# Gated attention and its feed-forward on one core: the values computed transposed, with V as the loaded weight and the squares streamed

## The chip, the cores and the metric

The kernel runs on one core of a Trainium2 chip. The metric is the time of one execution in microseconds (us) on the device; runs of the kernel before took 1242.19, 1242.97 and 1243.57 us, median 1242.97 us.

## What is computed

For each of 8 batches with S = 3008 rows, u and v have 256 columns and z has 64. The first half of the kernel makes x from them, the second half is a feed-forward over all 24064 rows of x:

```python
scores = (1.0 / S) * np.matmul(z, z.transpose(0, 2, 1))
attn = np.maximum(scores, 0.0) ** 2
x = u * np.matmul(attn, v)          # then as 24064 rows of 256
h = x @ w_in                        # 256 -> 2048
g = h * (1.0 / (1.0 + np.exp(-1.702 * h)))
out = g @ w_out                     # 2048 -> 256
```

All inputs and the output are float32; the kernel's products take float16.

## The kernel before, in words

**Tiles.** Each batch's rows are cut into NIS = 6 units of 512 query rows, 48 units in all; the last unit of a batch has only 448 rows (it is called short here). The key rows are cut into NJ = 24 blocks of 128. Every matmul has a contraction of 64: the 128 rows of the array are used as two halves of 64, which work on two matmuls at a time (a pair) and add into two PSUM banks, g = 0 and 1. The two banks are added later.

**Scores.** `scores` (L286) computes for a unit n and a pair t of key blocks the scores transposed: keys on the partitions, 512 queries along the row. `relu` (L335) takes them out of PSUM on ACT or DVE, `squared` (L315) squares them in place in float16, L318 on ACT or L320 on DVE. Since the scores are symmetric, from unit 3 on the squares for earlier key blocks are not computed again: they are earlier squares, turned by a DMA transpose (tiles T, L256), and part of the diagonal block comes likewise from a half block (`mirror`, L271).

**Values, before.** `values` (L444) multiplies squares and V: a block of squares, 128 keys by 128 queries, is the loaded weight, and 256 columns of V are streamed (L457). The result, O, has queries on the partitions. A unit has 24 key blocks, 4 blocks of queries and 2 halves of the array: 192 matmuls of 256 columns; h = 0 and 1 are the two pairs of query blocks. `halves` (L512) does the last key block. In a short unit the fourth query block has 64 rows; `shorts` (L524) does it with 128 rows by 64 columns of the array (L532), and the two halves of its result are joined by a small DMA (`two`, L506) and an add (L501).

**Out of PSUM.** `both_sums` (L424) copies the two banks into a tile `sums` (L436 on ACT or L438 on DVE; 3 such tiles rotate), POOL adds the two copies (L431). For O, POOL then multiplies with u (`gate`, L473) into X. X has rows on the partitions; the feed-forward needs it the other way round, so `turn_x` (L354) turns it with DMA transposes (L367, L374) into the ring XT, and `swap_x` (L378) copies it with its two partition halves exchanged into XS (L385).

**Feed-forward.** `hidden` (L537) makes 2 x 128 of the 2048 hidden columns for a block m of 512 rows with eight matmuls of 512 columns (L547) into hg; ACT's sigmoid (L554) and DVE's multiply (L558) make GT. `outs` (L574) multiplies GT by W2 (L585, 256 columns streamed) into yps, which leaves by `both_sums` too, and is stored (L602). hg and the scores share two PSUM tiles, tag A; O and yps share four banks, tags B00 to B11.

**Order.** The program is written out by a planner that runs when it is built: it keeps one clock for each engine (`now`), a table of assumed costs (`cost`, L138), and a list of PE work (`work`, L610: O of unit n, then yps of block n - 3). Scores and hg are put in between where an engine is free. Work for ACT and DVE goes to whichever the planner has earlier, POOL's to POOL; DMAs that SP issues wait in a list (`sends`) and go out in the order of their due unit. The resulting order on each engine is fixed: an instruction that waits holds all that stand behind it on its engine.

Of the kernel before, what the change touches and what calls it, by code (L numbers as in the profile page):

```python
# [9 lines left out]
F16 = mybir.dt.float16  # L10
P = 128
# [3 lines left out]
def kernel(  # L15
# [41 lines left out]
    NG = 8  # L57

# [20 lines left out]
    RU = [const.tile([P, NIB, D], F32, name=f"RU{i}") for i in range(2)]  # L79
    for i in range(2):  # L80
        pool.memset(RU[i][SREM:, NIB - 1, :], 0.0)

# [18 lines left out]
    def load_u(n):  # L101
        b, isup = divmod(n, NIS)
        rows(b, u, isup * NIB, (isup + 1) * NIB, RU[n % 2], sp, 1)

# [11 lines left out]
    def turn_z(b, q):  # L116
# [25 lines left out]
        ("sp", "turn"): 1.45, ("sp", "mirror"): 1.3, ("sp", "turn_x"): 2.6, ("sp", "turn_z"): 2.2, ("sp", "store"): 0.6, ("sp", "swap"): 1.2,  # L142
# [143 lines left out]
    def scores(k):  # L286

        nonlocal nxt
        for i in range(k):
# [25 lines left out]
            def squared(e, at, n=n, t=t, a=a, isup=isup, cols=cols):  # L315
# [5 lines left out]
                if isup == NIS - 1 and t == NP - 1:  # L321
                    pool.memset(a[:, 1, ISUP - SREM:], 0.0)
                    at += 0.5
# [25 lines left out]
    Os, Ys, GTs, Xs = {}, {}, {}, {}  # L349
# [4 lines left out]
    def turn_x(n, at):  # L354
        b, isup = divmod(n, NIS)
        X = Xs.pop(n)
        t0 = b * S + isup * ISUP
        end = min(t0 + ISUP, (b + 1) * S)
        for c in range(NK):
            k = 0  # L360
            while t0 + k < end:
                p0 = (t0 + k) % RING
                room = min(end - t0 - k, RING - p0)
                r0, blk = k % P, k // P
                if r0 == 0 and room >= P:
                    nb = room // P
                    sp.dma_start_transpose(  # L367
                        XT[:, c, p0:p0 + nb * P].rearrange("p (n t) -> p n t", t=P),
                        X[:, c, blk:blk + nb, :].rearrange("p n d -> p (n d)"),
                    )  # L370
                    k += nb * P
                else:
                    r = min(room, P - r0)
                    sp.dma_start_transpose(XT[:, c, p0:p0 + r].unsqueeze(1), X[r0:r0 + r, c, blk, :])  # L374
                    k += r
        send(at + T_DMA, "swap", n + 1, lambda at: swap_x(t0, end, at))
# [13 lines left out]
    def squares_of(n, j, ib):  # L390

        J = j // NIB
        if turned_from(n, J):
            return T[(n, J)][:, ib, j % NIB, :]
        a = A[(n, j // 2)]
        if mirrored(n, j // 2) and ib < NIB // 2:
            return a[:, 0, (2 * ib + j % 2) * P:(2 * ib + j % 2 + 1) * P]
        if J == n % NIS and n >= NMIR:
            return by_halves(a)[:, j % 2, ib // 2, ib % 2 * P:(ib % 2 + 1) * P]
        return a[:, j % 2, ib * P:(ib + 1) * P]  # L400
# [20 lines left out]
    def take_banks(h, name):  # L421
        set_bank(h, None)
        return [psB.tile([P, 2, D], F32, name=f"{name}{g}{h}", tag=f"B{g}{h}") for g in range(2)]

    def both_sums(ps, h, scale, at, then):

        s_ = pb.tile([P, 2, 2, D], F32, name="sums", tag="sums", bufs=3)
        done = []

        def add(e, at):  # L430
            pool.tensor_tensor(s_[:, 0, :, :], s_[:, 0, :, :], s_[:, 1, :, :], ALU.add)  # L431
            then(s_[:, 0, :, :], at)

        def leave(g, e, at):
            if e == "act":
                act.activation(s_[:, g, :, :], ps[g], AF.Copy, scale=scale)  # L436
            else:
                dve.tensor_scalar(s_[:, g, :, :], ps[g], scale, None, ALU.mult)  # L438
            done.append(at)
            if len(done) == 2:  # L440
                set_bank(h, max(done))
                push(max(done), "add", ("pool",), add)

        for g in range(2):  # L444
            push(at, "part", BOTH, lambda e, at, g=g: leave(g, e, at))

    def values(n, js, h, ends):
        V = V16[n // NIS % 2]
# [3 lines left out]
        short = h == 1 and n % NIS == NIS - 1  # L452
        for j in js:
            for i2 in range(1 if short else 2):
                sq = squares_of(n, j, 2 * h + i2)
                for g in range(2):
                    pe.matmul(  # L457
                        O[g][:, i2, :], half(sq, g), half(V[:, j, :], g),
                        start=(j == 0 and i2 == 0), stop=(ends and j == js[-1] and (i2 == 1 or short)),
                    )  # L460
        at = pe_at(H, T_MM * (1 if short else 2) * len(js))
        if h == 1 and (not short or js[0] >= NJ - TAIL):
            for j in js:
                drop(n, j)
        if ends:
            if h == 0:
                assert n - 2 not in Xs
                Xs[n] = pb.tile([P, NK, NIB, P], F16, name="X", tag="X")
            O, X, R = Os.pop((n, h)), Xs[n], RU[n % 2]
            both = None  # L470

            def gate(ib, k, p=P):
                pool.tensor_tensor(  # L473
                    X[:p, :, ib:ib + k, :].rearrange("p c n d -> p n c d"),
                    both[:p, ib - 2 * h:ib - 2 * h + k, :].rearrange("p n (c d) -> p n c d", c=NK),
                    R[:p, ib:ib + k, :].rearrange("p n (c d) -> p n c d", c=NK),
                    ALU.mult,
                )

            def gone(at):  # L480
                if h == 1:
                    send(at, "turn_x", n, lambda at: turn_x(n, at))
                    if n + 2 < NU:
                        send(at, "store", n + 1, lambda at: load_u(n + 2))

            def summed(s_, at):
                nonlocal both
                both = s_
                if not short:
                    def mul(e, at):  # L490
                        gate(2 * h, 2)
                        gone(at)

                    push(at, "gate", ("pool",), mul)
                    return


                two = pb.tile([H, D], F32, name="two", tag="two", bufs=1)

                def add(e, at):  # L500
                    pool.tensor_tensor(both[:H, 1, :], both[:H, 1, :], two, ALU.add)  # L501
                    gate(3, 1, H)
                    gone(at)

                def move(at):
                    sp.dma_start(two, both[H:, 1, :])  # L506
                    push(at + 2.0, "gate", ("pool",), add)

                push(at, "gate", ("pool",), lambda e, at: gate(2, 1))
                send(at, "store", 0, move)  # L510

            both_sums(O, h, 1.0, at, summed)  # L512

    def halves(n):

        V = V16[n // NIS % 2]
        for q in range(NIB // 2):
            for g in range(2):
                pe.matmul(  # L519
                    Os[(n, g)][g][:, q, :], half(squares_of(n, NJ - 1, 2 * g + q), g), half(V[:, NJ - 1, :], g),  # L520
                    start=False, stop=False,
                )
        pe_at(H, 2 * T_MM)
        drop(n, NJ - 1)  # L524

    def shorts(n):

        V = V16[n // NIS % 2]
        O = Os[(n, 1)][0]
        for j in range(NJ - 1):  # L530
            c0 = j % 2 * SREM
            pe.matmul(  # L532
                O[c0:c0 + SREM, 1, :], squares_of(n, j, NIB - 1)[:, :SREM], V[:, j, :],
                start=False, stop=False, tile_position=(0, c0),
            )
        pe_at(0, T_MM * NJ / 2)
        for j in range(NJ - TAIL):  # L537
            drop(n, j)
# [27 lines left out]
    def last_out(Y, r0):  # L566

        o = pb.tile([P, 2, 2, D], F32, name="sums", tag="sums", bufs=3)
        for i2 in range(2):
            act.activation(o[:, 1, i2, :], Y[1][:, i2, :], AF.Copy, scale=1.0 / FSC)  # L570
            dve.scalar_tensor_tensor(o[:, 0, i2, :], Y[0][:, i2, :], 1.0 / FSC, o[:, 1, i2, :], ALU.mult, ALU.add)
            sp.dma_start(out[(r0 + i2) * P:(r0 + i2 + 1) * P, :], o[:, 0, i2, :])

    def outs(m, fg, h):  # L574
# [6 lines left out]
        for e, i2 in [(x, y) for x in range(2) for y in range(2)] if not end else [(0, 0), (1, 0), (0, 1), (1, 1)]:  # L581
            ff = fg + e * NFG
            s = 2 * h + i2
            for g in range(2):
                pe.matmul(  # L585
                    Y[g][:, i2, :], half(GT[:, e, s * P:(s + 1) * P], g), half(W2[:, ff, :], g),
# [5 lines left out]
        if end:  # L592
# [7 lines left out]
            def summed(s_, at):  # L600
                def store(at):
                    sp.dma_start(out.rearrange("(n p) c -> p n c", p=P)[:, r0:r0 + 2, :], s_)  # L602
# [4 lines left out]
            both_sums(Y, h, 1.0 / FSC, at, summed)  # L607
# [4 lines left out]
    for n in range(NTB + LAG):  # L612
        m = n - LAG
        if n < NU:
# [6 lines left out]
            for h in range(2):  # L621
                for j in range(NJ - TAIL, NJ - 1):
                    if j == NJ - 2 and h == 0:
                        work.append(("r", n, [NJ - 1]))
                        if n % NIS == NIS - 1:
                            work.append(("s", n, list(range(NJ - 1))))
# [5 lines left out]
    spans = {"r": 2 * T_MM, "s": T_MM * NJ / 2, "y": 4 * T_MM}  # L632
    before = [0.0]
    due = {}
    for i, w in enumerate(work):
        before.append(before[-1] + (2 * T_MM * len(w[2]) if w[0] == "o" else spans[w[0]]))
# [17 lines left out]
    at(0, 12, lambda: load_u(0))  # L654
    at(0, 13, load_w1, lambda: load_u(1))
# [154 lines left out]
```

## Time and profile before

| what | value |
|---|---|
| time, median of 3 runs | 1242.97 us |
| the profiled execution's own time | 1240.06 us |
| its span, first to last instruction | 1238.1 us |
| granted TensorE clock | 0.999 |
| PE busy | 1219.2 us, 18600 matmuls |
| PEld (weight loads) busy | 1018.0 us |
| DVE, ACT, POOL busy | 908.7, 810.3, 476.0 us |
| DMA: moved, mean rate | 167.25 MB, 135 GB/s |

The span lies 2 us inside the profiled execution's time, and that lies 2.9 us below the median. The busy time of a matmul is modelled and contains its latency (a pair overlaps), so that the pace of PE is read from the starts of matmuls, or from the chain of work, not from the mean of one.

### The profile page before, as it was taken

The numbers are of one execution on the slowest core, as the hardware profiler recorded it, in microseconds if no ns is written. First come the engines' busy times: TensorE is split into PE (matmuls) and PEld (weight loads), VectorE is DVE, ScalarE is ACT, GpSimd is POOL, SyncE is SP. The second block draws the span as 40 slices with busy tenths as digits, with TensorE's granted clock in tenths as the row PEclk, the third lists the DMA queues.
The fourth block names the chain that finished last, engine by engine and source line by source line (L and its number), as shares of the span: only waits on it lengthen the run. The fifth ranks groups of instructions, "written<-read, shape, count | busy, mean of one in ns | idle before, by whom it ended". The sixth has DMA issues, their size and how long they took to land.

```text
span 1238.1 us, 42078 instructions
## 1 busy us (share of the span) xinstructions
PE 1219.2 (98%) x18600; PEld 1018.0 (82%) x18600; DVE 908.7 (73%) x891; ACT 810.3 (65%) x948; POOL 476.0 (38%) x489
## 2 busy tenths in 40 slices
PE   8898999999999999999999999999999999999998
PEld 6787988887888878888988887888878888988886
DVE  8966777667876778767787677876777777777656
ACT  8865776566666666666666676666766666666544
POOL 5533343423443243433444333433434333422331
PEclk9999999999999999999999999999999999999999
DMA  9999797976888669795699946989559985685511
GB/s 166 167 169 167 139 139 137 165 125 117 142 162 153 109 117 146 132 191 105 117 148 178 144 96 125 156 128 179 103 115 172 164 132 109 134 155 100 97 45 60
DMA packets 465654, 167.25 MB, mean 135 GB/s; under 512 B 375360, under 2 KB 465472, under 8 KB 465472
## 3 DMA queue, kind: packets, MB, share of 16 engines
q1 hardware_dynamic: 414048, 147.14, 65.2%
q0 software_dynamic: 51424, 17.44, 14.0%
q8 instruction: 145, 2.38, 0.8%
q14 instruction: 37, 0.30, 0.1%
HBM read 60.29 MB, written 24.64 MB: 69 GB/s over the span
## 4 chain that ended last, share of the span: by engine, by line
PE 88%; DVE 1%; ACT 1%; issue 1%; DVEq 0%
PE O L457 33%; PE hg L547 25%; PE yps L585 24%; PE sc L301 4%; PE O L532 1%; PE O L519 1%; DVE GT L558 0%; DVE ap__6020 L320 0%; DVE ap__18204 L320 0%; DVE ap__12112 L320 0%; DVE sums L438 0%; DVE ap__21289 L339 0%; DVE ap__3546 L339 0%; DVE ap__9105 L339 0%; DVE ap__15197 L339 0%
## 5 line engine op out<-in xcount | busy, mean ns | idle before, releaser
L558 DVE TENSOR_TENSOR GT<-hg,tsg 128x1024 f16<-128x1024 f32 x376 | 453.6, 1219 | 220.4 <-ACT tsg L554 215.7
L554 ACT ACTIVATE tsg<-hg 128x1024 f16<-128x1024 f32 x376 | 378.3, 1022 | 283.6 <-PE hg L547 279.7
L431 POOL TENSOR_TENSOR sums<-sums 128x512 f32<-128x512 f32 x188 | 248.7, 1325 | 681.2 <-DVE sums L438 431.1
L547 PE MATMUL hg<-XT,W 64*128 64x512 f16 x1504 | 383.5, 376 | 2.3 <-DVE GT L558 2.0
L585 PE MATMUL yps<-W,GT 64*128 64x256 f16 x6016 | 380.8, 269 | 4.7 <-ACT sums L436 3.7
L547 PE MATMUL hg<-XS,W 64*128 64x512 f16 x1504 | 367.7, 376 | 0.0
L585 PEld LDWEIGHTS <-GT 64*128 64x128 f16 x6016 | 327.0, 94 | 42.8 <-issue 4.4
L547 PEld LDWEIGHTS <-W 64*128 64x128 f16 x3008 | 174.7, 94 | 88.8 <-issue 3.0
L457 PE MATMUL O<-V,T 64*128 64x256 f16 x3392 | 217.0, 269 | 0.0
L457 PEld LDWEIGHTS <-T 64*128 64x128 f16 x3392 | 185.9, 94 | 24.3
L473 POOL TENSOR_TENSOR X<-sums,RU 128x512 f16<-128x512 f32 (+2 forms) x104 | 138.7, 1334 | 7.5
L301 PE MATMUL sc<-ZT 64*128 64x512 f16 (+1 forms) x688 | 122.3, 363 | 5.4 <-DVE ap__832 L339 1.7
L436 ACT ACTIVATE sums<-yps 128x512 f32<-128x512 f32 x115 | 66.0, 594 | 38.9 <-PE yps L585 29.4
L436 ACT ACTIVATE sums<-O 128x512 f32<-128x512 f32 x110 | 63.3, 596 | 33.1 <-PE O L457 24.2
L438 DVE TENSOR_SCALAR sums<-O 128x512 f32<-128x512 f32 x82 | 55.6, 685 | 20.6 <-issue 9.9
L438 DVE TENSOR_SCALAR sums<-yps 128x512 f32<-128x512 f32 x69 | 47.4, 687 | 14.7 <-issue 10.1
L301 PEld LDWEIGHTS <-ZT 64*128 64x128 f16 x688 | 40.0, 94 | 12.1 <-issue 8.2
L87 POOL DMA_DIRECT2D V<-in_v_dram x32 | 28.0, 877 | 0.0
L119 POOL COPY z<-z 128x384 f16<-128x384 f16 x28 | 13.8, 493 | 0.0
L87 POOL DMA_DIRECT2D z<-in_z_dram x7 | 10.9, 1563 | 1.0 <-issue 1.0
L532 PE MATMUL O<-V,T 128*64 128x256 f16 x160 | 10.3, 275 | 0.0
L532 PEld LDWEIGHTS <-T 128*64 128x64 f16 x160 | 8.1, 110 | 1.7 <-issue 1.7
(1538 smaller groups left out, 1474.6 us busy)
## 6 DMA issues: line engine op xcount, KB each, us to landing
out_dram<-sums SPq DMA_DIRECT2D x92, 256.0 KB, 4.2
RU<-in_u_dram SPq DMA_DIRECT2D x40, 512.0 KB, 4.5
V<-in_v_dram POOLq DMA_DIRECT2D x24, 384.0 KB, 7.3
XS<-XT SPq DMA_DIRECT2D x60, 128.0 KB, 4.1
RU<-in_u_dram SPq DMA_DIRECT2D x8, 384.0 KB, 3.7
z<-in_z_dram POOLq DMA_DIRECT2D x7, 368.0 KB, 8.9
V<-in_v_dram POOLq DMA_DIRECT2D x8, 320.0 KB, 8.3
XT<-X SPq DMA_TRANSPOSE x144, 2.5
```

Source lines behind the costliest of these rows:

```text
L87: eng.dma_start(dst[:, :full - lo, :], dram[b, lo * P:full * P].rearrange("(n p) d -> p n d", p=P),)
L301: pe.matmul(sc[:, g, cols], Z[h0:h0 + DQK, 2 * t + g, :], Z[h0:h0 + DQK, isup * NIB + low:(isup + 1) * NIB, :], start=True, stop=True,)
L431: pool.tensor_tensor(s_[:, 0, :, :], s_[:, 0, :, :], s_[:, 1, :, :], ALU.add)
L436: act.activation(s_[:, g, :, :], ps[g], AF.Copy, scale=scale)
L438: dve.tensor_scalar(s_[:, g, :, :], ps[g], scale, None, ALU.mult)
L457: pe.matmul(O[g][:, i2, :], half(sq, g), half(V[:, j, :], g), start=(j == 0 and i2 == 0), stop=(ends and j == js[-1] and (i2 == 1 or short)),)
L473: pool.tensor_tensor(X[:p, :, ib:ib + k, :].rearrange("p c n d -> p n c d"), both[:p, ib - 2 * h:ib - 2 * h + k, :].rearrange("p n (c d) - ...
L532: pe.matmul(O[c0:c0 + SREM, 1, :], squares_of(n, j, NIB - 1)[:, :SREM], V[:, j, :], start=False, stop=False, tile_position=(0, c0),)
L547: pe.matmul(hg[:, e, :], half(W1[:, fg // 2, c, fg % 2 * P:(fg % 2 + 1) * P], e), half(x[:, c // 2, p0:p0 + TB], e), start=(c == 0), stop= ...
L554: act.activation(tsg, hg, AF.Sigmoid, scale=1.702 / FSC)
L558: dve.tensor_tensor(GT, hg, tsg, ALU.mult)
L585: pe.matmul(Y[g][:, i2, :], half(GT[:, e, s * P:(s + 1) * P], g), half(W2[:, ff, :], g), start=(fg == 0 and e == 0 and i2 == 0), stop=(end ...
```

## The change

The product is written the other way round. V is the loaded weight now: for a key block j and a half h of V's columns, 128 columns of V are loaded, and the squares of all the unit's queries are streamed, 512 wide. So h now stands for a half of the columns, and O has columns of V on its partitions and queries along the row: x transposed. The multiplication with u writes straight into the ring XT; `turn_x` and X are gone, `swap_x` stays. In a short unit 448 queries are streamed, and `shorts`, `two` and the memset of the padding are gone. Where the unit's squares do not lie in one pattern, they are streamed in two pieces, each with its own weight load (256 + 256 on the diagonal, 384 + 64 from the tiles T of a short unit, 256 + 192 on the diagonal of a short unit).

u must be transposed for this and is float32, while the DMA transpose takes 16-bit elements. So POOL splits each unit's u into its low and high 16-bit halves (`split_u`), two DMA transposes turn them (`turn_u`), and POOL puts them together again (`merge_u`). One tile of each kind exists; `u_did` has each step wait for the one before it and for its tile: load n for split n - 1; split n for load n and turn n - 1; turn n for split n and merge n - 1; merge n for turn n and the multiplication (gate) n - 1. The `sums` tiles become 4.

```diff
+    NSUM = 4
-    RU = [const.tile([P, NIB, D], F32, name=f"RU{i}") for i in range(2)]
+    RU = const.tile([P, NIB, D], F32, name="RU")
+    UH = const.tile([P, 2, NIB * D], U16, name="UH")
+    UHT = const.tile([P, 2, NIB, NK, P], U16, name="UHT")
+    UT = const.tile([P, NK, ISUP], F32, name="UT")
...
+    def split_u(n):
+        for w in range(2):
+            pool.tensor_copy(UH[:, w, :], RU.bitcast(U16).rearrange("p n (x w) -> p w (n x)", w=2)[:, w, :])
+
+    def turn_u(n):
+        for w in range(2):
+            sp.dma_start_transpose(UHT[:, w, :, :, :].rearrange("p n c r -> p (n c) r"), UH[:, w, :])
+
+    def merge_u(n):
+        for w in range(2):
+            pool.tensor_copy(
+                UT.bitcast(U16).rearrange("p c (n r w) -> p w n c r", n=NIB, w=2)[:, w, :, :, :], UHT[:, w, :, :, :],
+            )
...
-        ("sp", "turn"): 1.45, ("sp", "mirror"): 1.3, ("sp", "turn_x"): 2.6, ("sp", "turn_z"): 2.2, ("sp", "store"): 0.6, ("sp", "swap"): 1.2,
+        ("sp", "turn"): 1.45, ("sp", "mirror"): 1.3, ("pool", "split"): 2.2, ("pool", "merge"): 2.2, ("sp", "turn_u"): 2.9, ("sp", "turn_z"): 2.2, ("sp", "store"): 0.6, ("sp", "swap"): 1.2,
...
-    def turn_x(n, at):
...
-    def squares_of(n, j, ib):
+    def squares_of(n, j):
+        J, g, w = j // NIB, j % 2, width(n)
         if turned_from(n, J):
-            return T[(n, J)][:, ib, j % NIB, :]
+            t = T[(n, J)][:, :, j % NIB, :]
+            return [t] if w == ISUP else [t[:, :w // P, :], t[:, w // P, :w % P]]
...
+    def add_values(O, n, j, V, g, first, last):
+        c0 = 0
+        for k, x in enumerate(squares_of(n, j)):
+            w = x.shape[1] if len(x.shape) == 2 else x.shape[1] * x.shape[2]
+            o = O[:, c0:c0 + w]
+            yield o if len(x.shape) == 2 else o.rearrange("p (n r) -> p n r", n=x.shape[1]), V, half(x, g), first and c0 == 0, last and c0 + w == width(n)
+            c0 += w
...
         for j in js:
-            for i2 in range(1 if short else 2):
-                sq = squares_of(n, j, 2 * h + i2)
-                for g in range(2):
-                    pe.matmul(
-                        O[g][:, i2, :], half(sq, g), half(V[:, j, :], g),
-                        start=(j == 0 and i2 == 0), stop=(ends and j == js[-1] and (i2 == 1 or short)),
-                    )
+            both = [add_values(O[g], n, j, half(V[:, j, h * P:(h + 1) * P], g), g, j == 0, ends and j == js[-1]) for g in range(2)]
+            for pair in zip(*both):
+                for o, vj, x, first, last in pair:
+                    pe.matmul(o, vj, x, start=first, stop=last)
...
-            def gate(ib, k, p=P):
-                pool.tensor_tensor(
-                    X[:p, :, ib:ib + k, :].rearrange("p c n d -> p n c d"),
...
+                def gate(e, at):
+                    k = 0
+                    while k < w:
+                        p0 = (t0 + k) % RING
+                        r = min(w - k, RING - p0)
+                        pool.tensor_tensor(XT[:, h, p0:p0 + r], s_[:, k:k + r], UT[:, h, k:k + r], ALU.mult)
+                        k += r
+                    if h == 1:
+                        u_did("gate", n, at)
+                        send(at, "swap", n + 1, lambda at: swap_x(t0, t0 + w, at))
+
+                if u_done["merge"] >= n:
+                    push(at, "gate", ("pool",), gate)
+                else:
+                    waiting_gates.append((n, at, gate))
...
-    def shorts(n):
...
-    at(0, 12, lambda: load_u(0))
-    at(0, 13, load_w1, lambda: load_u(1))
+    at(0, 12, lambda: u_did("gate", -1, now["pe"]))
+    at(0, 13, load_w1)
```

## The prediction

> **What bounds the kernel now.** I read first the page's busy times, then the share by stages, then the waits of PE, then the chain of work inside one stage. The stages:
>
> ```profile
> PE 1219.2 (98%) x18600; PEld 1018.0 (82%) x18600; DVE 908.7 (73%) x891; ACT 810.3 (65%) x948; POOL 476.0 (38%) x489
> ```
>
> ```profile
> 0.00:60.00 60.00, 53.58 (x784) 44.12 (x785) 53.73 (x59) 50.63 (x57) 33.89 (x43) 1.00 1.23 168
> 60.00:130.00 70.00, 64.54 (x954) 52.32 (x955) 49.62 (x49) 41.02 (x49) 23.98 (x32) 1.00 1.02 165
> 130.00:1225.00 1095.00, 1093.38 (x16753) 915.81 (x16749) 799.23 (x778) 714.26 (x839) 418.15 (x415) 1.00 0.77 133
> ```
>
> Columns: PE, PEld, DVE, ACT, POOL busy, granted clock, DMA share, GB/s. From 130 us on PE never rests. Before that it rests 6.4 and 5.5 us; up to 60 us DVE is as busy as PE (53.7 of 60 us). So what PE streams counts in full, and a helper engine counts only where it makes PE wait. PE's waits, first up to 60 us, then from 60 to 130:
>
> ```profile
> PE sc L301 <- DVE ap__832 L339: 1.7, 1, 1.7
> PE sc L301 <- DVE ap__496 L339: 1.4, 1, 1.4
> ```
>
> ```profile
> PE yps L585 <- ACT sums L436: 3.7, 1, 3.7
> PE hg L547 <- DVE GT L558: 2.0, 2, 1.5
> ```
>
> The pace of PE, from the chain in a dense stage (start, length, matmuls), and its passage through `shorts`:
>
> ```profile
> 601.18 0.86 PE hg L547 x8
> 602.05 0.44 PE O L457 x8
> ```
>
> ```profile
> 278.79 1.43 PE O L532 x23
> ```
>
> Eight matmuls of 512 columns take 0.86 us, eight of 256 take 0.44; over all starts in the trace a pair of 512 takes 215.8 ns, a pair of 256 takes 109.2. That is 0.416 ns a column and 2.6 ns for each start.
>
> **Streaming, -6.8 us.** By the written order of the changed kernel its O takes 1740 pairs of 512, 7 of 448, 320 of 384, 320 of 64, 329 of 256 and 49 of 192 columns; before it was 4328 pairs of 256 and 184 matmuls of `shorts`. Where two pairs of 256 become one of 512, one start goes: 1740 x 2.6 ns = 4.5 us. In a short unit a key block costs 162.4 + 29.3 = 191.7 ns for each half of the columns; before it was 3.5 pairs for two halves, 191.1 each: nothing gained. But `shorts` takes 1.43 us where 23 x 54.6 ns = 1.26 are streamed, and by the starts there is another 0.1 us of standstill ahead of it: 0.28 us for each of 8 units, 2.3 us. Two costs are not in the trace. A matmul of 64 columns with its own weight load: a load is busy 94 ns, but wherever PE restarts after a wait the second load of a pair begins 1 ns after the first matmul and its own matmul 4 to 5 ns after that, so I take no cost beyond the stream; the far bound is a whole load not hidden, 65 ns on 320 pairs, +20.8 us. And a stream in four runs of 128 elements (tiles T, 1048 pairs), where every stream today is one run: I take nothing, since the nearest rows, 256 and 512, differ only by columns and starts; the bound is a start for each run, 3 x 2.6 ns x 1048 = +8.2 us. Neither can go below nothing: the columns and the starts are counted already.
>
> The Trainium skill, "TensorE: Matmul & The Clock Gate", section "Back-to-back issue gap", speaks against the narrow pieces: in a stream of load and matmul it gives about 81 ns per matmul at 128 columns. The trace has that stream: the 24 transposes of z (L689), 128 columns and a load each, start 53 to 56 ns apart. By the page's 81 ns a pair of 64 would lose at least 52 ns, 16.5 us on 320; by the row, nothing.
>
> **The stall at 101 us, -3.7 us.** PE's longest wait is for ACT, and ACT and DVE wait there 4.5 and 4.1 us for an out store: with three `sums`, O of h = 1 takes the tile of the yps just stored, and SP issued those stores late (100.3 us). With four, it takes a tile that a gate has freed a unit earlier. I count the 3.7 as gone.
>
> **POOL, +3 us in the long stage.** Added are 192 copies (two splits, two merges, 48 units) of 1024 elements; gone are 16 short adds and gates and 8 memsets. The rows:
>
> ```profile
> L431 POOL TENSOR_TENSOR sums<-sums 128x512 f32<-128x512 f32 x188 | 248.7, 1325 | 681.2 <-DVE sums L438 431.1 <-ACT sums L436 224.3 <-DMA T<-ap__21358 12.9
> L119 POOL COPY z<-z 128x384 f16<-128x384 f16 x28 | 13.8, 493 | 0.0
> L237 POOL COPY scrap<-V 1x2 f16<-1x2 f16 x2 | 0.3, 174 | 8.8 <-DVE V L320 7.7 <-ACT V L318 1.0
> ```
>
> From 174 ns for 2 elements and 493 for 384, a copy of 1024 takes 1.03 us; that it steps over every second half-word no row shows. From below it can't be under z's 0.49 us, from above at the two-input rate of L431 it is 2.48. I take 1.03, the row of the same kind: 198 us, POOL at some 54%. POOL's own time is hidden: XS of a block was issued 4 to 44 us ahead of its first hg. What isn't hidden is DVE's squares:
>
> ```profile
> L320 DVE TENSOR_TENSOR GT<-GT 128x1024 f16<-128x1024 f16 x4 | 2.6, 680 | 0.0
> L320 DVE TENSOR_TENSOR ap__736<-ap__736 128x1024 f16<-128x1024 f16 x1 | 1.8, 1758 | 0.0
> ```
>
> The same square, once alone, once beside POOL's work. The 54 squares that touch no POOL instruction average 0.689 us, all 179 take 169.3 us: 46 us more than alone, for 407 us of POOL arithmetic, 0.11 us for each. 198 us more make 22 us on DVE. DVE has that room (73% busy), but the two PSUM tiles of tag A are handed on closely: of 636 handovers after 130 us, 111 come less than 0.6 us before PE needs them, and 74 of these have a square in the 3.5 us before. So about 4 in 10 of the 22 us fall where it matters, and a third of it gets through the slack: +3 us; bounds 0 and, with copies of 2.48 us, +11.
>
> The Trainium skill, "SBUF — State Buffer", section "Who interferes with whom", says that VectorE with two SBUF inputs and GpSimd's reads exclude each other for a whole instruction. By that a square meets one of the 192 copies about 28 times (179 squares x 198 us / 1238) and waits half a copy, 15 us on DVE instead of 22: a third less of the term. The trace agrees in kind: DVE's multiply L558, one of whose inputs is PSUM, takes 1.21 to 1.23 us beside POOL or not.
>
> **The start, +4 us.** Up to 60 us DVE sets the pace and the DMA share is 1.23: transposes of T<-V and T<-GT take 8.3 us to land there. The first x now needs load, split, turn and merge of u in this stage. On SP, turn 0 stands behind the six T<-V, which ended at 33.8 us; landed at some 42 to 45, merged by 47. Behind the merge stand on POOL W2's load, split 1 (2.1 us) and the two gates (2.7): 53.3 us. XS(0) stands behind turn 1 on SP: issued at 54 against 47.5 us, landed after 4 to 5 us at 58 to 59, while the first hg came at 55.5. That is 3 us of wait. POOL is then busy almost to 72 us, and some four more squares slow by 0.8 us each; 1.7 us of this go into a wait that PE has at 59 us anyway. 3 + 3 - 1.7 makes 4; bounds -1 (transposes at the 4.0 us that they take on the median) and +12 (each of three units adds a landing of 4 us to POOL's chain).
>
> **The rest at nothing.** SP: 144 transposes of X (some 1.2 us to issue) and 8 small copies go, 96 of u (1.3 us, as T) come; behind them stand mirrors and T, and the mirrors have 7 to 32 us from issue to first use. DMA: 96 x 1024 packets of 256 bytes replace 48,000, and at 27 ns a packet 16 engines get 85 us more, a share of 0.84 instead of 0.77 in the long stage; if a T came late it would cost PE up to a landing, but PE waits for no DMA today. ACT and DVE copies keep their size. The end keeps its work; XS is ready sooner by the turn of X.
>
> **Sum.** 1240.06 - 4.5 - 2.3 - 3.7 + 3 + 4 = 1236.6 us for the profiled execution; that execution lies 2.9 us below the median of runs, so **1239.5 us**.
>
> **The rivals.** (A) Both added costs are hidden: squares slow only where DVE has room and merge 0 comes in time. Then 1240.06 - 10.5 + 2.9 = 1232.5. For it: PE doesn't wait for today's slowed squares after 130 us; against: the closeness of the handovers. (B) Costs and gains cancel: start and squares cost 10.5 us instead of 7, what the gains are: 1243. For it: both are terms of a chain that DVE and DMA already fill. (C) Slower: POOL becomes the brake, through the half-word copies. At 2.48 us each POOL has 476 us more, DVE 54; 11 us get through after 130 us, and the start costs 10, since the four copies ahead of the first gates are 1.45 us longer each: 1240.06 - 10.5 + 21 + 2.9 = 1253.5. It decides from about 1.8 us a copy. For it: no row shows such a copy; against: the copy row. (D) The narrow pieces pay a whole weight load: 1239.5 + 20.8 = 1260; against it the 4 to 5 ns after restarts. By the 81 ns of the Trainium skill ("TensorE: Matmul & The Clock Gate", "Back-to-back issue gap") the same rival would give 1256. (E) The streams in runs cost a start each: 1239.5 + 8.2 = 1247.7. That the change doesn't do what it says I rule out: the written order holds the counts above and no turn of X.
>
> **How the numbers follow.** Forecast, 1235 to 1240.5: 0.33. A, 1230 to 1235: 0.15. B, 1240.5 to 1245.5: 0.20. C: 0.21, D: 0.06, E: 0.05. A difference of 0.2%, 2.5 us, is about what a measurement of this kernel can tell from none. Faster 0.48 (forecast and A), same 0.20, slower 0.32. The forecast's own range is 1235 to 1240.5. The range of 8 in 10 runs from 1232, into A, to 1255, over C's price, and leaves out D and the rest of A and C.
>
> **What would show it.** Right: pairs of 512 at 216 ns for O and a chain with O x8 in 0.86 us; no wait of PE for `sums` near 100 us; copies at L112 and L120 of about 1.0 us; a wait of the first hg, near 55 us, for XS of some 3 us; more squares over 1 us. Wrong: copies of 2 us, O's 384 + 64 at more than 200 ns, waits of PE after 130 us above 6 us in all, or a first hg that doesn't wait.

## The result, and the profile after

The changed kernel takes 1263.9 us (median of 4 runs, 1263.0 to 1267.0), the kernel before beside it 1242.6 (1241.4 to 1243.6): the ratio is 1.0184, with a 95% interval of 1.0170 to 1.0197. It is 21 us slower, where 3 us faster was forecast, and beyond the range. The profiled execution took 1263.0 us, its span 1261.2.

The page of the changed kernel, busy times, and its three stages (columns as before: PE, PEld, DVE, ACT, POOL busy, clock, DMA share, GB/s):

```profile
PE 1222.4 (97%) x15290; PEld 849.7 (67%) x15290; DVE 943.0 (75%) x880; ACT 813.0 (64%) x959; POOL 705.3 (56%) x676
```

```profile
0.00:60.00 60.00, 51.46 (x430) 25.97 (x432) 52.41 (x55) 46.87 (x54) 30.45 (x40) 0.97 1.14 176
60.00:130.00 70.00, 68.89 (x870) 45.06 (x867) 50.51 (x47) 45.72 (x54) 48.40 (x50) 1.00 1.00 148
130.00:1225.00 1095.00, 1071.33 (x13560) 754.44 (x13556) 817.17 (x757) 701.97 (x831) 621.39 (x584) 1.00 0.81 143
```

From 130 us on PE was busy for all but 1.6 of 1095 us before; now it rests 23.7. The stage from 60 to 130 us, where the wait at 101 us stood, has become better (68.9 instead of 64.5). What PE waits for from 130 us on, the first lines of its waits:

```profile
PE O L510 <- DVE sums L490: 5.8, 10, 1.4
PE O L510 <- DMA ap__1838<-ap__1504: 5.4, 1, 5.4
PE hg L556 <- DVE ap__12675 L355: 1.7, 1, 1.7
PE hg L556 <- DVE ap__15321 L355: 1.7, 1, 1.7
```

One is a mirror's DMA, once. The others are DVE's: copies of `sums` (L490) and relus (L355). There are five waits of 1.7 us, a batch apart. DVE itself is busy only 75%.

The streaming is as forecast. PE's rows in the timeline, of the pieces of a short unit and of full blocks (start, length with latency, engine, line, operation, count at the end; the group of 24 holds 384 and 64 columns in turn):

```profile
430.90 1.33 PE L510 MATMUL O<-T,V 64*128 64x384 f16 x24
432.05 0.38 PE L556 MATMUL hg<-XT,W 64*128 64x512 f16 x1
...
621.95 1.04 PE L510 MATMUL O<-ap__9896,V 64*128 64x512 f16 x8
622.81 0.61 PE L510 MATMUL O<-ap__9900,V 64*128 64x512 f16 x4
```

Eight of 512 columns take 622.81 - 621.95 = 0.86 us. Twelve pairs of the pieces take 432.05 - 430.90 = 1.15 us, and 6 x (162.4 + 29.3) ns is 1.15: no weight load is paid, no run of a stream either. If every matmul is counted at 0.4164 ns a column and 2.6 ns a start, the streams sum to 1209.4 us before and 1204.9 after, the 4.5 us of the forecast. What the starts show beyond that sum (waits, and matmuls at a lower clock) I call **standstill**, below by stretches: 22.8 us before, 50.5 after. 27.7 - 4.5 = 23.2 us is the whole difference of the two profiled executions (22.9).

| kernel | median us | ratio to before, 95% | standstill 0-100 | 100-200 | 200-1200 | squares' excess 200-1200 |
|---|---|---|---|---|---|---|
| before | 1242.6 | | 10.6 | 6.0 | 4.6 | 36.0 |
| after | 1263.9 | 1.0170-1.0197 | 15.3 | 10.8 | 22.7 | 67.4 |
| e1_no_copies | 1234.1 | 0.9920-0.9952 | 14.5 | 0.0 | 4.3 | 34.8 |
| e2_late_merge | 1241.6 | 0.9976-1.0010 | 18.2 | 7.5 | 4.5 | 35.6 |
| e3_before_copies | 1246.8 | 1.0026-1.0056 | 11.8 | 7.3 | 8.6 | 64.4 |
| e4_before_4sums | 1236.6 | 0.9941-0.9971 | 10.8 | 1.8 | 4.3 | 35.4 |
| e5_scratch_merge | 1260.8 | 1.0151-1.0186 | 14.2 | 11.7 | 24.3 | 67.5 |
| e6_wait_only | 1242.3 | 0.9991-1.0018 | 10.3 | 9.1 | 4.4 | 35.5 |
| e7_two_loads | 1264.0 | 1.0177-1.0227 | 14.3 | 11.2 | 22.5 | 67.4 |
| e8_late_merge2 | 1240.8 | 0.9991-1.0014 | 13.8 | 6.8 | 4.5 | 35.3 |
| e9_early_loads | 1261.7 | 1.0144-1.0191 | 14.7 | 8.3 | 22.5 | 66.6 |
| e10_f16 | 1227.8 | 0.9866-0.9913 | 12.3 | 0.0 | 2.7 | 29.3 |
| e11_5sums | 1263.1 | 1.0147-1.0187 | 13.4 | 13.4 | 22.3 | 66.9 |
| e12_split_no_wait | 1256.2 | 1.0089-1.0126 | 13.8 | 5.4 | 26.0 | 67.3 |

The ratios are to runs of the kernel before on the same chip. The last column sums, over DVE's squares from 200 to 1200 us, what each takes beyond 0.689 us, the time of a full one alone (a half square, 0.43 us alone, counts only beyond 0.689 us too). The added copies, by POOL's groups:

```profile
L120 POOL COPY UT<-UHT 128x1024 uint16<-128x1024 uint16 x96 | 141.4, 1516 | 31.1 <-DMA UHT<-UH 28.3
L112 POOL COPY UH<-RU 128x1024 uint16<-128x1024 uint16 x96 | 98.1, 1048 | 34.4 <-DMA UHT<-UH 24.2 <-DMA RU<-in_u_dram 9.8
```

The splits take 1.05 us on the mean, near the 1.03 forecast. The merges take 1.34 us alone and 1.5 on the mean.

### The profile page after: what moved, and what is told of

It is laid out like the page before. It is cut to its first block, busy times and chain, and to the rows that moved or that the text cites. A ratio compares the mean times of both kernels' runs of the same rounds, so it can differ in the third digit from the quotient of the medians.

```text
span 1261.2 us, 35710 instructions
## 1 busy us (share of the span) xinstructions
PE 1222.4 (97%) x15290; PEld 849.7 (67%) x15290; DVE 943.0 (75%) x880; ACT 813.0 (64%) x959; POOL 705.3 (56%) x676
## 4 chain that ended last, share of the span: by engine, by line
PE 81%; DVE 6%; DMA 5%; POOL 4%; issue 3%; SPq 1%; ACT 1%; DVEq 0%; POOLq 0%
PE O L510 32%; PE hg L556 24%; PE yps L595 20%; PE sc L320 4%; DMA UHT<-UH 2%; DMA RU<-in_u_dram 1%; POOL UT L120 1%; POOL sums L483 1%; POOL XT L526 1%; PE O L545 1%; DVE GT L567 1%; DMA ap__1838<-ap__1504 1%; DVE sums L490 1%; POOL UH L112 1%; SPq L116 0%
## 5 line engine op out<-in xcount | busy, mean ns | idle before, releaser
L483 POOL TENSOR_TENSOR sums<-sums 128x512 f32<-128x512 f32 (+1 forms) x188 | 247.8, 1320 | 453.9 <-DVE sums L490 233.0
L510 PEld LDWEIGHTS <-V 64*128 64x128 f16 x5420 | 307.8, 94 | 199.2 <-issue 20.7
L556 PE MATMUL hg<-XS,W 64*128 64x512 f16 x1504 | 335.0, 376 | 0.0
L556 PEld LDWEIGHTS <-W 64*128 64x128 f16 x3008 | 189.1, 94 | 139.0 <-issue 13.4
L510 PE MATMUL O<-T,V 64*128 64x512 f16 (+2 forms) x2496 | 244.8, 314 | 4.4 <-DVE sums L490 4.4
L120 POOL COPY UT<-UHT 128x1024 uint16<-128x1024 uint16 x96 | 141.4, 1516 | 31.1 <-DMA UHT<-UH 28.3
L320 PE MATMUL sc<-ZT 64*128 64x512 f16 (+1 forms) x688 | 140.3, 365 | 6.0 <-DVE ap__641 L355 2.2
L526 POOL TENSOR_TENSOR XT<-sums,UT 128x512 f16<-128x512 f32 (+7 forms) x116 | 139.2, 1208 | 7.1
L112 POOL COPY UH<-RU 128x1024 uint16<-128x1024 uint16 x96 | 98.1, 1048 | 34.4 <-DMA UHT<-UH 24.2
L488 ACT ACTIVATE sums<-O 128x512 f32<-128x512 f32 (+1 forms) x130 | 72.8, 588 | 29.6 <-PE O L510 27.4
L490 DVE TENSOR_SCALAR sums<-yps 128x512 f32<-128x512 f32 x65 | 44.3, 681 | 12.7 <-POOL UT L120 7.5
L490 DVE TENSOR_SCALAR sums<-O 128x512 f32<-128x512 f32 (+1 forms) x62 | 41.4, 670 | 10.6 <-PE O L510 7.7
L138 POOL COPY z<-z 128x384 f16<-128x384 f16 x28 | 13.8, 492 | 0.0
```

The costliest lines, as they stand in the source:

```text
L112: pool.tensor_copy(UH[:, w, :], RU.bitcast(U16).rearrange("p n (x w) -> p w (n x)", w=2)[:, w, :])
L120: pool.tensor_copy(UT.bitcast(U16).rearrange("p c (n r w) -> p w n c r", n=NIB, w=2)[:, w, :, :, :], UHT[:, w, :, :, :],)
L320: pe.matmul(sc[:, g, cols], Z[h0:h0 + DQK, 2 * t + g, :], Z[h0:h0 + DQK, isup * NIB + low:(isup + 1) * NIB, :], start=True, stop=True,)
L483: pool.tensor_tensor(s_[:, 0, :w], s_[:, 0, :w], s_[:, 1, :w], ALU.add)
L488: act.activation(s_[:, g, :w], ps[g][:, :w], AF.Copy, scale=scale)
L490: dve.tensor_scalar(s_[:, g, :w], ps[g][:, :w], scale, None, ALU.mult)
```

## The experiments

**The theories.** T1: the copies slow DVE's squares, and what stands behind those in DVE's order (relus, copies of `sums`) reaches PE late; T1a by running beside the squares, T1b by holding POOL's queue in a wait. T2: the planner's new order is tighter by itself. T4: u's chain on POOL and SP makes the mirror late.

**e1_no_copies.** u is left out of the product.

```diff
     def split_u(n):
         for w in range(2):
-            pool.tensor_copy(UH[:, w, :], RU.bitcast(U16)...[:, w, :])
+            pass
...
-            pool.tensor_copy(UT.bitcast(U16)...[:, w, :, :, :], UHT[:, w, :, :, :])
+            pass
```

> The changed kernel with POOL's split and merge copies taken out: loads, turns and gates stay, and the order of every other engine's instructions is the same; u is left out of the product (the gate multiplies with ones). Theory T1 (the 192 copies slow DVE's squares, and relus and handovers come late): PE's standstill after 200 us falls from 22.7 to about 5 us and part of that before goes too, so 1263.9 - 18 to -24 = 1240 to 1246 us. Theory T2 (the planner's new order has tighter handovers, whatever POOL does): 1259 to 1265 us, as the changed kernel.

Measured 1234.1 us, 30 us below the changed kernel and 8 below the kernel before. T2 falls for the long stage: with the same order on PE, ACT and DVE the standstill there is 4.3 us. The gain exceeds T1's 18 to 24, since the standstill of 100 to 200 us went as well (10.8 to 0.0); that of the first 100 us stayed (14.5).

**e2_late_merge.** Only the place of the merges on POOL changes. As it turned out, the transpose of the next unit may be written ahead of such a merge, so that a unit is multiplied with the u of the next; the work is the same.

```diff
+    pending = []
+    def flush():
+        while pending:
+            put_together(pending.pop(0))
     def split_u(n):
+        flush()
...
     def merge_u(n):
+        pending.append(n)
+    def put_together(n):
...
                 def gate(e, at):
+                    if n in pending:
+                        flush()
```

> The changed kernel with the same copies, but each merge written just ahead of the next split (or ahead of its own gate, if that comes first) instead of right behind the gate of h = 1: only POOL's order changes. T1, in the form that the place counts (56 of 96 merges lie beside runs of squares, 67 us of overlap): 10 to 15 us faster than the changed kernel, 1249 to 1254 us. T1, in the form that only the amount of copies counts: 1260 to 1265. T2: 1260 to 1265.

Measured 1241.6 us: 22 us faster, more than the first form of T1 expected. The amount of copies is the same; their place is what costs.

**e3_before_copies.**

```diff
                         gate(2 * h, 2)
+                        if h == 1:
+                            for w in range(2):
+                                pool.tensor_copy(DB[:, :, w], DA)
```

> The kernel before with two copies added on POOL behind each gate of h = 1, of the merge's kind (1024 half-words written with a step of two, between two tiles that nothing else uses): half of the copies that the change adds, and no other instruction moved. T1: 10 to 18 us slower than before, 1253 to 1261 us. T2 (the order costs, the copies don't): 1242 to 1244 us.

Each unit of 512 rows gets two copies, 80 in all; the short units' gates stand at another place and get none, so that this is less than the half of the change's 192 that the expectation speaks of. Measured 1246.8 us: 4.4 us slower (3.2 to 7.0 by the interval), beyond T2's nothing, but less than half of what T1 expected. The window from 200 to 1200 us, first of the kernel before, then of e3:

```profile
200.00:1200.00 1000.00, 998.74 (x15331) 831.86 (x15327) 729.33 (x710) 651.06 (x765) 380.46 (x376) 1.00 0.78 133
```

```profile
200.00:1200.00 1000.00, 996.70 (x15258) 832.14 (x15256) 754.35 (x709) 651.66 (x765) 472.45 (x439) 1.00 0.77 133
```

DVE is as busy as in the changed kernel (below), the squares are slowed as much (28 us more than before), and yet PE loses only 4 us of them there. So slowed squares are a condition, not yet a price. With e1 this makes a square of four kernels in the long stage: 4.6 us of standstill before, 8.6 with copies alone (e3), 4.3 with the new order alone (e1), 22.7 with both. Neither the copies nor the order costs the 18 us by itself.

**e4_before_4sums.**

```diff
-        s_ = pb.tile([P, 2, 2, D], F32, name="sums", tag="sums", bufs=3)
+        s_ = pb.tile([P, 2, 2, D], F32, name="sums", tag="sums", bufs=4)
```

> The kernel before with 4 sums tiles instead of 3, nothing else. The prediction's step (PE's wait of 3.7 us near 101 us goes with the fourth tile): 1238 to 1240 us and no wait of PE for sums near 101 us. Rival (the wait is taken over by the next late thing, as the changed kernel has as much standstill from 100 to 200 us): 1241 to 1244 us.

Measured 1236.6 us, 5.7 us faster (3.6 to 7.3): the step of the prediction holds, and a little more. From 95 to 110 us, where PE waited 3.7 us for `sums`, its waits are now this one:

```profile
PE hg L547 <- DVE GT L558: 0.3, 1, 0.3
```

**e5_scratch_merge and e6_wait_only** part T1a from T1b: e5 keeps the time of a merge and drops its wait, e6 keeps the wait and drops its time.

```diff
 e5
-                UT.bitcast(U16)...[:, w, :, :, :], UHT[:, w, :, :, :],
+                DB.bitcast(U16)...[:, w, :, :, :], UH[:, w, :].rearrange(...),
 e6
-                UT.bitcast(U16)...[:, w, :, :, :], UHT[:, w, :, :, :],
+                UT.bitcast(U16)[:, 0, w:w + 1], UHT[:, w, 0, 0, :1],
```

> The changed kernel with each merge copy put to a scratch tile: same shape, same step of two half-words in the write, same place on POOL, but it reads UH, which is long written, so that it waits for no transpose; u is left out of the product (the gate multiplies with ones). All other engines' orders are unchanged. Theory T1a (the copies slow the squares by running beside them): PE's standstill from 200 to 1200 us stays at 15 us or more, 1255 to 1264 us. Theory T1b (the merges hold POOL's queue while they wait for the transposes, 28 us in all, so that adds and gates behind them come late): standstill from 200 to 1200 us falls to about 5 us, 1240 to 1247 us.

> The changed kernel with each merge copy cut to one half-word per partition: it waits for the transpose at the same place but takes no time to speak of; u is left out of the product (the gate multiplies with ones). T1a (running beside the squares): 1240 to 1249 us. T1b (holding POOL's queue): 1255 to 1264 us.

Measured 1260.8 and 1242.3 us: T1a. The merges' waits for their transposes, 28 us on POOL, cost nothing in the long stage. The window from 200 to 1200 us says it in one line for each kernel (PE, PEld, DVE, ACT, POOL busy): the changed kernel, e5, and e6.

```profile
200.00:1200.00 1000.00, 984.23 (x12411) 693.98 (x12409) 753.85 (x696) 647.73 (x766) 561.18 (x532) 1.00 0.81 143
```

```profile
200.00:1200.00 1000.00, 984.22 (x12386) 692.28 (x12384) 753.56 (x696) 647.52 (x766) 560.65 (x531) 1.00 0.81 142
```

```profile
200.00:1200.00 1000.00, 997.46 (x12744) 634.32 (x12742) 731.62 (x705) 654.95 (x777) 477.48 (x530) 1.00 0.81 142
```

The copies' time puts 22 us on DVE, and PE is 13 us less busy for it.

**e7_two_loads.**

```diff
-    RU = const.tile([P, NIB, D], F32, name="RU")
+    RU = [const.tile([P, NIB, D], F32, name=f"RU{i}") for i in range(2)]
```

> The changed kernel with two RU tiles, as before the change, instead of one, and nothing else: a load of u no longer waits on SP for the split of the unit before. Theory T4 (the mirror that PE awaits at 138.8 us stood on SP behind a load that waited for a split): that wait of 5.5 us and the slow clock behind it, 2 us, go: 1255 to 1258 us. Rival (the mirror stood behind the turns and the traffic in any case): 1261 to 1266 us.

Measured 1264.0 us: nothing gained, PE waits even 7.3 us for the mirror. This form of T4 falls. SP's order shows why: the load no longer waits for the split, but behind it a swap waits for a gate (10.2 us).

**e8_late_merge2.** e2's place of the merges, with two UHT tiles, so that each unit gets its own u.

```diff
+    UHT = [const.tile([P, 2, NIB, NK, P], U16, name=f"UHT{i}") for i in range(2)]
```

> The changed kernel with the merges written as late as in e2_late_merge, and with two UHT tiles, so that each merge gets its own unit's u. If the place of the merges is what costs: standstill from 200 to 1200 us about 5 us instead of 22, 1240 to 1247 us. If e2's gain came from elsewhere (its merges read the tile of the next unit's transpose, so that nothing on SP waited as it does here): 1255 to 1264 us.

Measured 1240.8 us, 23 us faster than the changed kernel with all of its work done. The second UHT tile isn't the reason, since e2 gains the same with one: it is the place of the merges. Only 9 of 96 merges meet a square now, 62 in the changed kernel. Its window:

```profile
200.00:1200.00 1000.00, 997.48 (x12744) 634.66 (x12740) 732.25 (x705) 654.56 (x777) 547.77 (x533) 1.00 0.81 142
```

POOL is as busy as in the changed kernel (547.8 against 561.2), DVE as idle as without merges. How it goes shows best in the timeline of one unit. The changed kernel, DVE and POOL together:

```profile
448.40 1.62 DVE L339 TENSOR_TENSOR ap__7289<-ap__7289 128x1024 f16<-128x1024 f16 x1
...
449.53 3.36 POOL L120 COPY UT<-UHT 128x1024 uint16<-128x1024 uint16 x2
...
449.94 1.76 DVE L339 TENSOR_TENSOR ap__7304<-ap__7304 128x1024 f16<-128x1024 f16 x1
...
451.62 1.76 DVE L339 TENSOR_TENSOR ap__7328<-ap__7328 128x1024 f16<-128x1024 f16 x1
...
453.31 1.21 DVE L355 TENSOR_SCALAR ap__7379<-sc 128x1024 f16<-128x1024 f32 x1
```

The same instructions of DVE in e8, with no copy there:

```profile
440.90 1.62 DVE L349 TENSOR_TENSOR ap__7290<-ap__7290 128x1024 f16<-128x1024 f16 x1
442.44 0.68 DVE L349 TENSOR_TENSOR ap__7305<-ap__7305 128x1024 f16<-128x1024 f16 x1
443.04 0.68 DVE L349 TENSOR_TENSOR ap__7329<-ap__7329 128x1024 f16<-128x1024 f16 x1
443.64 1.21 DVE L365 TENSOR_SCALAR ap__7378<-sc 128x1024 f16<-128x1024 f32 x1
```

When the gate of h = 1 is done, the planner lets DVE square what has gathered, five squares in a row. Adds and gates have already slowed the first three in both kernels, by 2.1 us together; the two merges bring it to 4.3 us, and the relu behind them comes 4.9 us after the third square's start instead of 2.7. This one relu is late by more than its PSUM tile's slack, and PE waits 1.7 us for it. In e8 that slack can be read: the relu ends at 443.64 + 1.21 = 444.85 us, and PE starts on its tile at 445.20, 0.35 us later. The two merges add 2.1 us. Summed over runs of squares (those less than 2.5 us apart) the profile has, from 200 to 1200 us, five of 4.3 us of excess in the changed kernel and none over 2.1 before; e3 has six of 3.2 us. Some 3 us of excess in one run are mostly absorbed; what comes on top goes to PE. That runs of squares set the price I read from these timelines; no run varied their length.

**e9_early_loads.**

```diff
 (with e7's two RU tiles)
-        if ask("load", n_, ("split", n_ - 1)):
+        if ask("load", n_, ("split", n_ - 2)):
```

> The changed kernel with two RU tiles (as in e7_two_loads) and each load of u asked for one unit earlier, so that no split waits for a load. T4 in its second form (the mirror that PE awaits near 137 us stands on SP behind a swap that waits for a gate, and that gate stands on POOL behind a split that waits 5.7 us for its load): that wait of PE and the slow clock behind it go, 7 to 9 us: 1255 to 1258 us. Rival (the mirror is late by the transfers themselves): 1261 to 1266 us.

Measured 1261.7 us (1259.4 to 1265.2): no decision. The edit missed its aim: the next load still left SP only at 110 us, behind the transposes of u that wait for a split, and the split on POOL waited 10.3 us for it instead of 5.7. PE's wait for the mirror was 4.2 us.

**e11_5sums.**

```diff
-    NSUM = 4
+    NSUM = 5
```

> The changed kernel with 5 sums tiles instead of 4, nothing else. If part of the loss goes by way of sums (DVE's copies out of PSUM wait 7.5 us for a tile that POOL's adds and gates, held behind the merges, have not freed): 4 to 6 us faster, 1257 to 1260 us. If it goes by way of the slowed squares alone: 1262 to 1266 us.

Measured 1263.1 us, with 22.3 us of standstill in the long stage: the second case. DVE's 7.5 us of waiting for a `sums` tile is no part of the loss there.

**e12_split_no_wait.** u is left out; constants are split, turned and merged.

```diff
-            pool.tensor_copy(UH[:, w, :], RU.bitcast(U16)...[:, w, :])
+            pool.tensor_copy(UH[:, w, :], RX.bitcast(U16)...[:, w, :])
```

> The changed kernel with the splits reading a constant tile instead of RU: same copies in the same places, but no split waits for a load of u (and no load for a split); u is left out (constant ones are split, turned and merged). T4 in its third form (POOL stands still in a split that waits for its load, 5.7 us near 120 us, and gate, swap and store, and the mirror behind them on SP, are late by that): the wait of PE near 137 us and the slow clock behind it go, standstill from 100 to 200 us falls from 10.8 to 2 to 4 us, and the long stage stays at 18 to 23: 1255 to 1258 us. Rival (the splits' own 2 us of POOL and the transfers make the mirror late, not the wait): 10 us of standstill from 100 to 200 us stay, 1261 to 1266 us.

Measured 1256.2 us, 7.8 below the changed kernel: T4's third form, though not all of its numbers. The wait for the mirror is gone; a new one of 1.9 us, and the slow clock behind it, near 112 us leaves 5.4 us of standstill from 100 to 200 us instead of the expected 2 to 4. The long stage came to 26.0 us, above the 18 to 23 expected; PE's waits there are those of the changed kernel, but the granted clock is 0.98 instead of 1.00 from 400 to 500 us and from 600 to 700, and why is open. In the changed kernel the cause reads, on POOL and then on SP:

```profile
125.59 2.02 POOL L112 COPY UH<-RU 128x1024 uint16<-128x1024 uint16 x2 [5.72 <-DMA RU<-in_u_dram]
127.57 1.26 POOL L526 TENSOR_TENSOR XT<-sums,UT 128x512 f16<-128x512 f32 x1
```

```profile
116.87 11.14 SPq L92 DMA_DIRECT2D RU<-in_u_dram  x2
128.86 1.29 SPq L422 DMA_DIRECT2D XS<-XT  x2
130.26 3.11 SPq L116 DMA_TRANSPOSE UHT<-UH  x2
133.43 1.84 SPq L612 DMA_DIRECT2D out_dram<-sums  x2
136.83 0.38 SPq L92 DMA_DIRECT2D RU<-in_u_dram  x1
137.26 1.21 SPq L290 DMA_TRANSPOSE ap__1838<-ap__1504  x1
```

A load issued at 116.9 us, among the loads of V for the second batch, has not landed before 125.6. Split, gate, swap, turn, store and load follow each other across the two queues, and the mirror that PE needs at 138.8 us is issued last, at 137.3.

**e10_f16**, the version that the experiments pointed to: no copy at all.

```diff
-    RU = const.tile([P, NIB, D], F32, name="RU")
-    UH = ...
-    UHT = ...
-    UT = const.tile([P, NK, ISUP], F32, name="UT")
+    RU = [const.tile([P, NIB, D], F16, name=f"RU{i}") for i in range(2)]
+    UT = [const.tile([P, NIB, NK, P], F16, name=f"UT{i}") for i in range(2)]
...
-        rows(b, u, isup * NIB, (isup + 1) * NIB, RU, sp, 1)
+        rows(b, u, isup * NIB, (isup + 1) * NIB, RU[n % 2], pool, 1)
...
-        for w in range(2):
-            sp.dma_start_transpose(UHT[:, w, :, :, :].rearrange("p n c r -> p (n c) r"), UH[:, w, :])
+        sp.dma_start_transpose(UT[n % 2].rearrange("p n c r -> p (n c) r"), RU[n % 2].rearrange("p n d -> p (n d)"))
```

> The changed kernel with u cast to float16 by its load (issued by POOL, as V's), turned by one transpose and multiplied from there: no split and no merge, two tiles of each kind; the orders of PE, ACT and DVE are unchanged. u is rounded to 16 bits, which x is anyway. T1a (the copies beside squares are the loss): standstill as without copies, 1229 to 1237 us, at or below e1_no_copies (1234). Rival (48 more loads issued by POOL cost the squares as much as the copies did): 1245 us or more.

Measured 1227.8 us (1226.2 to 1231.8), a little below the range of T1a: 36 us faster than the changed kernel, 14.6 faster than the kernel before (ratio 0.989, 0.9866 to 0.9913), and faster than e4. It also drops the splits' waits and some of the traffic (DMA share 0.77 instead of 0.81), so that not all of the gain is the copies'. Its window:

```profile
200.00:1200.00 1000.00, 999.05 (x12813) 640.99 (x12809) 727.21 (x706) 657.47 (x780) 412.73 (x448) 1.00 0.77 122
```

## Why the prediction was wrong, step by step

- **Streaming, -6.8.** The stream's 4.5 us are there: the pairs start at the pace that was counted. The 2.3 us of `shorts` are not shown. They are a standstill that can't be told from the others in the changed kernel; in the long stage e10 stands still 1.9 us less than before, but e1, which has no `shorts` either, only 0.3. Rivals D and E are out: pieces and runs cost nothing. The 81 ns at 128 columns of the Trainium skill ("TensorE: Matmul & The Clock Gate", "Back-to-back issue gap") do not hold for these pairs, whose pieces of 64 columns take 29 ns.
- **The stall at 101 us, -3.7.** Right: e4 alone brought 5.7 (3.6 to 7.3).
- **POOL, +3 in the long stage: this step failed.** It measured +18.1 (22.7 against 4.6). Two parts of it were near: 239.5 us of copies instead of 198, and 31 us more on DVE's squares instead of 22. What failed is "about 4 in 10 of the 22 us fall where it matters, and a third of it gets through", 13%: 18.1 of 31.4 is 58%. The share came from the handovers of the kernel before, and there it is right: e3 adds 28 us to its squares, and 4.0 us, 14%, get through.
- **Why the share didn't carry over** to the changed kernel's order. Its copies are not spread evenly over DVE's squares, as I had it: 62 of 96 merges meet squares, for 69 us in all, but only 5 of 96 splits do, for 2 us, since the merges stand right behind the gate of h = 1, which is where DVE's runs of squares are. But that alone isn't the difference: e3's copies stand behind that gate too, and 51 of 80 meet squares. What differs is how closely the tiles of tag A are handed on. From 200 to 1200 us, PE takes such a tile less than 0.2 us after the instruction that frees it has ended in 12 of 579 handovers before, but in 56 of 581 in e1 and 42 of 583 in e8, where the squares are slowed no more than before. I never looked up, in the written order, what DVE does while POOL merges and what stands behind it. That the closer handovers set the share agrees with these counts; no run varied them alone. The count of handovers isn't borne out either: by the same measure, 411 of the kernel before's 636 after 130 us come less than 0.6 us ahead of PE, not 111. Of these just 111 are freed by DVE and taken by scores, while the five waits of 1.7 us are hg's.
- **Rival C** named the mechanism with another trigger, copies of 1.8 us or more; at 1.34 us the place was enough.
- **The Trainium skill on the squares**, "SBUF — State Buffer", "Who interferes with whom": of VectorE with two inputs from SBUF and a GpSimd instruction that reads SBUF, whichever comes second waits out the other's instruction. The trace agrees in kind: beside a merge a square takes 1.76 us instead of 0.68. Which came second it doesn't show: in the last section a square that starts 0.08 us ahead of an add, by the recorded starts, still ends after it. The estimate of 28 squares that meet a copy took the copies for evenly spread; 72 of 181 squares met one.
- **The start, +4.** It measured +4.7 up to 100 us, but not by the step's path, so that the near number is luck: in this profile the first hg waits for no XS. That wait of 1.9 to 3.9 us is there in e1, e5, e6 and e9, when other delays don't come first. Here DVE's squares were held from 25.8 us on (last section): PE waited 1.6 us for one of them and 2.2 us for a relu. e1, without copies, loses as much (14.5 in all), e6 loses nothing (10.3): which of POOL's instructions meets which square differs from kernel to kernel, and what would mend the start stays open.
- **The rest at nothing: this failed too**, for the mirrors, which "have 7 to 32 us from issue to first use". One was issued 1.5 us ahead, at the cost of 5.4 us and of a slower clock (0.95 from 130 to 200 us). With the 3.7 us gained there, 100 to 200 us came out 8.5 us above the forecast. e12's median is 7.8 us lower; in its profile this stretch gives 5.4 back. I had counted SP's own issue times and landings, and not that POOL, waiting in a split, would hold the gate and with it SP.
- **Sum.** 15.1 (POOL) + 8.5 (100 to 200 us, the mirror above all) + 0.7 (start) + 2.3 (`shorts`, inside these standstills) = 26.6 us; the forecast of 1236.6 for the profiled execution missed 1263.0 by 26.4.

## What to carry to other kernels

The price of slowing an engine is not its added busy time by a mean share: look up in the written order what it does at the very moment when the new work runs beside it, whether several slowed instructions stand in a row ahead of one that PE waits for, and how much slack that one has in the new order, not in the old. A copy on an engine with room (POOL is 56% busy) can be moved by a few microseconds for nothing; here that was worth 23 us. And a step that waits for a load belongs behind, not ahead of, the work that other queues wait for.

## What the runs showed of the hardware that was not expected

- A square on DVE can be held over more than one of POOL's instructions. In the changed kernel's timeline, DVE and POOL:

```profile
25.80 3.20 DVE L339 TENSOR_TENSOR ap__358<-ap__358 128x1024 f16<-128x1024 f16 x1
...
25.88 2.56 POOL L483 TENSOR_TENSOR sums<-sums 128x512 f32<-128x512 f32 x2
```

The square, 0.69 us alone, ended at 29.00 us, 0.56 us after the second add. In the long stage no square takes more than 1.77 us. Relus, whose input is PSUM, take 1.21 to 1.23 us beside POOL too.

- A copy of 1024 half-words on POOL takes 1.04 us when it steps over half-words in its read (L112) and 1.34 when it steps in its write (L120; e3's copies, which step in the write alone, take 1.34 too).
- POOL's issue of a load did not hold squares: in e10 squares that overlap only with it took 0.67 to 0.69 us (at 41.2 and 43.0 us for two).
